# Rows of two token blocks turned by VectorE and a DRAM scratch, and five unused products in the first quad

## The chip, the cores and the metric

The kernel runs on one core of one Trainium2 chip. Its engines are TensorE (PE; the loading of its weights is shown apart as PEld), VectorE (DVE), ScalarE (ACT), GpSimd (POOL) and SyncE (SP), which only issues DMAs here. Each engine works through its own queue in the order in which the program was written for it. The metric is device time in microseconds (us) of one execution, and the median of several runs.

## The reference

One transformer block on 2048 tokens of width 576, in float32: adaptive LayerNorm, grouped attention with 32 query heads of 18 and one shared key and value head, then a channel MLP of 4608.

```python
mod = (_silu(c) @ w_mod).reshape(c.shape[0], 6, 1, -1)
sa, ca, ga, sb, cb, gb = (mod[:, 0], mod[:, 1], mod[:, 2], mod[:, 3], mod[:, 4], mod[:, 5])
h = _layernorm(x, axis=-1) * (1 + ca) + sa
x = x + ga * _A_ref(h, A_wq, A_wk, A_wv, A_wo)
h = _layernorm(x, axis=-1) * (1 + cb) + sb
x = x + gb * _B_ref(h, B_w1, B_b1, B_w2, B_b2)
```

`_A_ref` projects h to 32 query heads, one key head and one value head, takes softmax of the scores times 18 ** -0.5, and projects the result; `_B_ref` is LayerNorm, a dense layer, GELU and a second dense layer.

## The kernel before

The order of the instructions is written out by hand (`manual_schedule`): what stands in the program for an engine is run in that order, and waits on other engines are put in by semaphores. There are three parts: projections of q, k and v (up to about 128 us), attention (to about 1370 us) and the MLP. The change is in the first part and at the head of the second.

**First part.** The 2048 tokens are four blocks `tb` of 512, each of four tiles `t` of 128 tokens. LayerNorm of a tile is done by `ln1_stats` (DVE statistics, three small POOL rows) and `ln1_apply` (ACT or DVE writes the normalised tile to Z, 128 tokens x 576). The projection needs h with the 576 channels on the partitions: five groups `k` of 128 channels (the last one has 64, held twice). `h_chunk(tb, zt, k)` turns four 128x128 pieces of Z with four PE transposes into a psB buffer, and `h_evac` scales them: ACT writes `hf`, ACT writes the rounded high part (`big<-hf`), and POOL or DVE the low part. A product is taken in three terms (high x high, low x high, high x low), so a `q_chunk` of 126 or 128 output columns is 14 products of 512 columns (`proj`).

A block has five such chunks, in the order m = 4, 0, 1, 2, 3 (`i` = 0 to 4). Behind each chunk ACT copies psB to `qf` and `qs`, POOL makes the low part of `qs`, and SP stores it to DRAM (`qscr`). m = 4 holds v and k; behind m = 0 the block's keys and values are finished (`k_block`, `v_block`). The block loop places other work at each `i`:

- h of the next block: `h_chunk` of k = 0, 1, 2 behind `i` = 1 and of k = 3, 4 behind `i` = 2 (in block 0 behind 3 and 4);
- normalising ahead (`NAPPLY`): block 2's tiles 0 and 1 at the end of block 0 and 2 and 3 behind block 1's `i` = 0; block 3's tiles 0 and 1 behind block 1's `i` = 3, and 2 and 3 behind `i` = 4;
- score products of quad 0 for its row maxima (`smax_part`), which are called in the middle of a chunk (`mid`): two psA buffers get two products each, and DVE takes their maxima (L346).

psB has three buffers in this part and psA two; Z has one.

**Second part.** It goes over 32 quads (4 heads x 512 tokens). In each quad scores are taken (`S0`, `S1`, L962), ACT takes their exponential (L964), the value products are summed (`V`, L952, into psC), and for the next quad row maxima are taken (`M0`, `M1`, L321 into three psM buffers, then DVE L984). The strings QUAD, QUADW and LAST fix the order of these tokens. In the first quad the first `LAG` = 8 quarter steps of V have no value products to do, since these follow the exponentials by two steps; so nothing but S and M stands there. Groups 0 and 1 use rows 0 to 63 and 64 to 127 of the array.

Of the kernel before, what the change touches and what calls it, by code (L numbers as in the profile page):

```python
# [8 lines left out]
F32 = mybir.dt.float32  # L9
# [5 lines left out]
S, D, H, DH, F = 2048, 576, 32, 18, 4608  # L15
NB = 4
TB = S // NB
NT = TB // 128
KD = 5
# [13 lines left out]
def block_kernel(ctx: ExitStack, tc, x, wqkv, wo, w1, b1, w2, b2, c, wmod, ident_in, out):  # L33
    nc = tc.nc
    ve, ac, po, pe, sy = nc.vector, nc.scalar, nc.gpsimd, nc.tensor, nc.sync

    per = ctx.enter_context(tc.tile_pool(name="per", bufs=1))
    dr = ctx.enter_context(tc.tile_pool(name="dr", bufs=1, space=bass.MemoryType.DRAM))
# [14 lines left out]
    def psB(): return PS["t"].tile([128, 512], F32, name="psB", bufs=PS["b"])  # L53
    def psC(): return PS["t"].tile([128, 512], F32, name="psC", bufs=1)

    open_ps("1", 3)
    def big(): return per.tile([128, 10, 512], F32R, name="big", bufs=3)
# [10 lines left out]
    w2sum = dr.tile([NG, 128, 4, 2, 288], F32, name="w2sum")  # L68
    turned = [dr.tile([D, 128], F32, name="turned%d" % n) for n in range(2)]
    turned0 = dr.tile([D, 128], F32, name="turnedA")  # L70
    qscr = dr.tile([NB, 2, H * DH, TB], F32, name="qscr")


# [11 lines left out]
    KS = pa.tile([128, S], F32R, name="KS")  # L85
# [3 lines left out]
    p1 = ph1.__enter__()  # L89
# [66 lines left out]
    def tr(o, Z, k):  # L156
        pe.transpose(o, Z[:, 128 * k:128 * (k + 1)], ident)
# [14 lines left out]
    Zs = {}  # L172
# [10 lines left out]

    def ln1_apply(tb, t, e):
        if t == 0:
            Zs[tb] = p1.tile([128, NT, 640], F32, name="Z1")
        Z = Zs[tb]
        X = XT[:, NT * tb + t, :]
        rs, nb = RN.pop((tb, t))
        for o, i in ((Z[:, t, :D], X), (Z[:, t, D:], X[:, 512:])):  # L190
            if e is ac:
                ac.activation(o, i, AF.Identity, scale=rs, bias=nb)
            else:
                ve.tensor_scalar(o, i, rs, nb, op0=ALU.mult, op1=ALU.add)

    mcol = p1.tile([128, 2, KD], F32, name="mcol")

# [29 lines left out]
    def h_evac(p, zt, k, e, first=False):  # L227

        hf = p1.tile([128, TB], F32, name="hf", bufs=3)
        ac.activation(hf, p, AF.Identity, scale=mcol[:, 1, k:k + 1], bias=mcol[:, 0, k:k + 1])  # L230
        if first:
            ve.tensor_copy(zt[:, k, :], hf)
        else:
            ac.activation(zt[:, k, :], hf, AF.Copy)
        e.tensor_tensor(zt[:, KD + k, :], hf, zt[:, k, :].bitcast(F32), op=ALU.subtract)

    def h_chunk(tb, zt, k):
        p = psB()
        for t in range(NT):
            tr(p[:, 128 * t:128 * (t + 1)], Zs[tb][:, t, :], k)  # L240
        h_evac(p, zt, k, ve if tb == 1 and k in (1, 3, 4) else po, tb == 1 and k < 3)

    def proj(o, wh, wl, c0, c1, zt, mid=None, n=0):
# [28 lines left out]
    def q_chunk(tb, m, zt, mid, n):  # L272

        w = 126 if m < KD - 1 else 128
        wd = 126 if m < KD - 1 else 72
        pq = psB()
        proj(pq[:w], wqh, wql, 126 * m, 126 * m + w, zt, mid, n)
        qs = p1.tile([128, 2, TB], F32R, name="qs", bufs=2)
        qf = p1.tile([128, TB], F32, name="qf", bufs=2)
        ac.activation(qf[:w], pq[:w], AF.Copy)  # L280
        ac.activation(qs[:w, 0], pq[:w], AF.Copy)
        po.tensor_tensor(qs[:w, 1], qf[:w], qs[:w, 0].bitcast(F32), op=ALU.subtract)
        if m == KD - 1:
            if tb >= 2:
                key_diff(tb, qf)
        sy.dma_start(qscr[tb, :, 126 * m:126 * m + wd, :].rearrange("s p t -> p s t"), qs[:wd].bitcast(F32))
        return qf, qs

    def k_block(tb, qs):

        pk = psB()
        for i in range(2):
            pe.matmul(pk, pick[:, i, :], qs[:, i, :], start=(i == 0), stop=(i == 1))
        ac.activation(KS[:, TB * tb:TB * (tb + 1)], pk, AF.Identity, bias=ones)

    def v_block(tb, qf):
        pk = psB()
        for i in range(NT):
            pe.transpose(pk[:, 128 * i:128 * (i + 1)], qf[:, 128 * i:128 * (i + 1)], ident)
        ve.tensor_copy(V[:, NT * tb:NT * (tb + 1), :DH],  # L300
                       pk.rearrange("p (i c) -> p i c", i=NT)[:, :, 72:72 + DH])
# [68 lines left out]
    for t in range(NT):  # L370
        ln1_stats(0, t)
        if t:
            ln1_apply(0, t - 1, ve if t % 2 else ac)
# [31 lines left out]
    def dense(n, w, x):  # L405

        p = psB()
        for _ in range(n):
            pe.matmul(p, w, x, start=True, stop=True)
# [35 lines left out]
    def unit():  # L445
        nonlocal u1
        smax_half(1, u1 % 2, u1 // 2)
        u1 += 1
# [5 lines left out]
    for tb in range(NB):  # L454
        nz = big() if tb + 1 < NB else None
        for i, m in enumerate((4, 0, 1, 2, 3)):
            np_ = NPART[tb][i]
            if i == 2:
                parts.extend((u, tb) for u in range(8))
            mid = {(NB - 1, 1): unit, (NB - 1, 4): lambda: last.popleft()()}.get((tb, i), part)  # L460
            qf, qs = q_chunk(tb, m, zt, mid, np_ + 1 if np_ else 0)
            if i == 0:
                qv = qf, qs
            if i == 1:
                k_block(tb, qv[1])
                v_block(tb, qv[0])
                if tb == 0:
                    load_q(0)
            if i == 2:
                if tb == 0:  # L470
                    load_q(1)
            if tb == NB - 1:
                if i == 0:
                    unit()
                elif i == 3:
                    smax_fin1(0)
                if i == 4:
                    dense(5, wqh[:, 0, :128], KS[:, :512])
                    unit()
                    dense(4, wqh[:, 0, :128], KS[:, :512])  # L480
            if nz is not None:
                for k in {1: (0, 1, 2), 2: (3, 4)}.get(i, ()) if tb else {3: (0, 1, 2), 4: (3, 4)}.get(i, ()):
                    h_chunk(tb + 1, nz, k)
            if tb < 2:
                for _ in range(NAPPLY[tb][i]):
                    b, t = applies.popleft()
                    ln1_apply(b, t, ve if b == 1 and t % 2 else ac)
                for _ in range(NSTAT[tb][i]):
                    ln1_stats(*stats.popleft())
        zt = nz  # L490
# [422 lines left out]
    LAG = 8  # L913
# [95 lines left out]

    part = deque((0, 1))  # L1010
    pq = 0
    for n in range(NQT):
        ns = [0, 0]
        if n < NQT - 1:
            order = QUADW if n > NQ else QUAD
        else:
            order = LAST
        if n < NQT - 1:
            kf, kr = (sum(int(tok[1]) for tok in order[:order.index(a)] if tok[0] == "V") // 4 for a in ("F2", "RC"))
            quiet = kf - 2, kf - 1, kr - 1  # L1020
        for tok in order:
            if tok[0] == "V":
                g = int(tok[1:])
                while g:
                    i = min(g, 4 - pq % 4)
                    if pq >= LAG:
                        pv_mm(*divmod((pq - LAG) // 4, 16), pq % 4, pq % 4 + i)
                    pq, g = pq + i, g - i
                    if pq % 4 == 0:
                        between(*divmod(pq // 4 - 1, 16))  # L1030
            elif tok[0] == "S":
                g = int(tok[1])
                two = sum(ns) % 7 % 2 if n == NQT - 1 else ns[g] % 2 and n == NQT - 2 and ns[g] > 24
                st_mm(n, ns[g] // 2, g, ns[g] % 2, psM if two else psB)
                ns[g] += 1
            elif tok in maxima:
                unit = next(maxima[tok], None)
                if unit:
                    mx_mm(*unit, tok[0], int(tok[1]))
            elif tok == "WO":  # L1040
                wo_next(psB)
            elif tok == "WP":
                h2 = part.popleft()
                p = psB()
                wo_mm(NB - 1, 2, h2, p, 0, KD - 1, KD - 1)
                wo_add(NB - 1, 2, h2, p)
            elif tok == "RW":
                for i, w in enumerate("hl"):
                    sy.dma_start(WO[w][:, KD - 1, :].bitcast(F32), woscr[i])
            elif tok[0] == "F":  # L1050
                (smax_fin1 if tok == "F1" else smax_fin2)(n + 1)
            elif n:
                if next(posts[0], 0) == 0:
                    posts.pop()
        if n == NQT - 1:
            W1["r"] = per.tile([128, 40, 128], F32R, name="w1a", tag="big", bufs=3)
            load_w1(0, " ".join(OPS) + " tails")
# [482 lines left out]
```

## Time and profile before

| | |
|---|---|
| runs | 2213.18, 2213.26, 2213.31 us; median 2213.26 |
| the profiled execution | 2214.96 us, with a span of 2212.9 us from its first to its last instruction |
| granted TensorE clock, mean | 0.998 |
| DMA packets | 233528, 317.67 MB |

The profile names a group of instructions by line, engine, operation and tiles (out<-in). In a timeline a row is start, duration, line, what is done and how often, and in brackets the idle time ahead of it and what ended it. In a table of stretches a row gives the stretch, its length, and for each engine the busy time (instructions), then the granted TensorE clock, the mean busy share of the 16 DMA engines, and GB/s.

### The profile page before, as it was taken

The page shows a single profiled execution, that of the slowest core. Times are in us where ns is not written, and L with a number is a line of the kernel's source. Part 1 is how long each engine was busy: PE and PEld are TensorE (multiplying, and loading weights), DVE is VectorE, ACT ScalarE, POOL GpSimd, SP SyncE. Part 2 cuts the span into 40 slices and gives each one's busy share as a digit, 9 for nine tenths or more (in the row PEclk, how much of TensorE's full clock was granted, in tenths as well). Part 3 has the DMA queues.
Part 4 walks back from the last instruction along what each step waited for, and adds up shares of the span by engine and source line. Part 5 has one row for each costly group of instructions (what it writes and reads, how often), then busy time and mean ns, then how long its engine had stood idle before and what let it go on. Part 6 is the DMA issues. An engine that isn't in the chain of part 4 may idle for free.

```text
span 2212.9 us, 46091 instructions
## 1 busy us (share of the span) xinstructions
PE 2193.5 (99%) x16559; PEld 1441.7 (65%) x16559; DVE 1935.3 (87%) x3421; ACT 1626.0 (73%) x3114; POOL 1520.2 (69%) x1760
## 2 busy tenths in 40 slices
PE   8999999999999999999999999999999999999999
PEld 6654445454544445444454445898988899889898
DVE  7589999999999999999999992888888878787887
ACT  5569999999999999999999998544445444343443
POOL 7654356667777677678675640888899767877776
PEclk9999999999999999999999999999999999999999
DMA  6232143333433443443343321666767746676664
GB/s 228 88 134 93 34 132 119 132 128 114 138 124 128 127 138 103 126 141 117 122 128 124 125 71 59 200 195 190 201 186 202 208 131 179 184 217 189 178 183 124
DMA packets 233528, 317.67 MB, mean 144 GB/s; under 512 B 58351, under 2 KB 124287, under 8 KB 233301
## 3 DMA queue, kind: packets, MB, share of 16 engines
q1 hardware_dynamic: 233157, 314.59, 46.4%
q8 instruction: 131, 2.15, 0.4%
q14 instruction: 96, 0.79, 0.1%
q10 hardware_dynamic: 144, 0.15, 0.0%
HBM read 205.92 MB, written 98.51 MB: 138 GB/s over the span
## 4 chain that ended last, share of the span: by engine, by line
PE 93%; DVE 1%; ACT 1%; issue 0%; ACTq 0%; DVEq 0%
PE psC L952 24%; PE psB L1176 18%; PE psA L1279 16%; PE psB L962 14%; PE psM L321 13%; PE psB L751 2%; PE psB L972 2%; PE psA L1313 1%; PE psA L751 1%; PE psB L250 0%; PE psB L359 0%; PE psM L962 0%; ACT P L964 0%; DVE mx L346 0%; DVE gs L1188 0%; ACT h L1185 0%
## 5 line engine op out<-in xcount | busy, mean ns | idle before, releaser
L964 ACT ACTIVATE P<-psB 128x512 f32<-128x512 f32 x2013 | 1055.6, 621 | 49.0 <-PE psM L321 24.4
L984 DVE TENSOR_REDUCE mx<-psM 128x1 f32<-128x512 f32 x1476 | 930.5, 681 | 27.6 <-PE psM L321 12.9
L962 PE MATMUL psB<-qst,KS 64*128 64x512 f32 x2013 | 604.8, 434 | 0.1
L321 PE MATMUL psM<-KS,qst 64*128 64x512 f32 x1722 | 594.0, 435 | 0.7 <-DVE mx L339 0.3
L952 PE MATMUL psC<-P,V 128*32 128x256 f32 (+3 forms) x6608 | 569.0, 440 | 0.0
L962 PEld LDWEIGHTS psB<-qst,KS 64*128 64x128 f32 x2013 | 302.1, 184 | 215.7 <-ACT P L964 184.6
L321 PEld LDWEIGHTS psM<-KS,qst 64*128 64x128 f32 x1722 | 285.4, 184 | 190.1 <-DVE mx L984 140.9
L1176 PE MATMUL psB<-ops,w1a 128*128 128x512 f32 x1512 | 393.9, 396 | 0.2 <-DVE h L1191 0.2
L1176 PEld LDWEIGHTS psB<-ops,w1a 128*128 128x128 f32 x1512 | 270.1, 188 | 46.8 <-DVE h L1191 0.6
L952 PEld LDWEIGHTS psC<-P,V 128*32 128x32 f32 x6608 | 147.1, 108 | 188.5 <-issue 160.9
L1285 DVE TENSOR_TENSOR XT<-psA,XT 128x576 f32<-128x576 f32 x330 | 241.2, 751 | 16.4 <-PE psA L1279 11.0
L1279 PEld LDWEIGHTS psA<-w2s,big 128*128 128x128 f32 x1584 | 223.6, 188 | 12.1 <-DVE XT L1285 0.2
L1279 PE MATMUL psA<-w2s,big 128*128 128x288 f32 x1584 | 230.1, 294 | 0.0
L1253 POOL TENSOR_TENSOR big<-s,big 128x512 fp32r<-128x512 f32 x132 | 170.9, 1295 | 10.6
L982 DVE CUSTOM_DVE_ANT_0 xc<-psM,xc 128x512 f32<-128x512 f32 x246 | 165.6, 680 | 11.8 <-PE psM L321 4.5
L1185 ACT ACTIVATE h<-psB,b1t 128x512 f32<-128x512 f32 x144 | 97.9, 680 | 105.7 <-PE psB L1176 99.3
L1189 ACT ACTIVATE psB<-gs 128x512 f32<-128x512 f32 x144 | 86.7, 602 | 119.9 <-DVE gs L1188 119.9
L975 ACT ACTIVATE xc<-psB 128x512 f32<-128x512 f32 x246 | 154.3, 627 | 5.5 <-PE psM L321 1.9
L788 POOL TENSOR_TENSOR os<-O,os 128x512 fp32r<-128x512 f32 x31 | 39.8, 1285 | 169.6 <-ACT os L787 169.5
L1188 DVE SCALAR_TENSOR_TENSOR gs<-psB,h 128x512 f32<-128x512 f32 x144 | 98.7, 686 | 38.7 <-ACT psB L1186 38.6
L822 POOL TENSOR_TENSOR r<-r,r 128x256 fp32r<-128x256 f32 (+1 forms) x162 | 121.8, 752 | 13.0
L1194 ACT ACTIVATE big<-h 128x512 fp32r<-128x512 f32 x39 | 24.7, 634 | 139.5 <-DVE h L1191 139.5
(215 smaller groups left out, 3289.2 us busy)
## 6 DMA issues: line engine op xcount, KB each, us to landing
w1a<-w1scr SPq DMA_DIRECT2D x252, 256.0 KB
w2s<-w2sum SPq DMA_DIRECT2D x132, 288.0 KB
w1scr<-r SPq DMA_DIRECT2D x126, 256.0 KB
w2s<-w2scr SPq DMA_DIRECT2D x76, 288.0 KB
w2scr<-r SPq DMA_DIRECT2D x72, 288.0 KB
w2sum<-r SPq DMA_DIRECT2D x72, 288.0 KB
qst<-qscr SPq DMA_DIRECT2D x192, 72.0 KB
w1a<-w2scr SPq DMA_DIRECT2D x33, 288.0 KB
```

Source lines behind the costliest of these rows:

```text
L321: pe.matmul(o, QST[n][64 * g:64 * g + 64, p, 128 * qt:128 * (qt + 1)], KS[64 * g:64 * g + 64, 512 * kb:512 * (kb + 1)], start=True, stop=True)
L822: po.tensor_tensor(o[:, n:2 * n], src, o[:, :n].bitcast(F32), op=ALU.subtract)
L952: pe.matmul(PVt[n][32 * j:32 * (j + 1), cs], V[:, kc, :], t[:, j, cs], start=(kc == 0 and h0 == 0), stop=(kc == 15), skip_group_check=True)
L962: pe.matmul(t, KS[64 * g:64 * g + 64, 128 * kc:128 * (kc + 1)], QST[n][64 * g:64 * g + 64, i, :], start=True, stop=True)
L964: ac.activation(P[n, kc][:, 2 * i + g, :], t, AF.Exp, scale=SCALE)
L975: ac.activation(XC[-1], t, AF.Relu)
L982: ve.tensor_tensor_reduce(c, t, c, 1.0, -3.0e38, ALU.add, ALU.max, o)
L984: ve.tensor_reduce(o, t, axis=AX.X, op=ALU.max)
L1176: pe.matmul(o, x, y, start=(first and i == 0), stop=(i == len(terms) - 1), skip_group_check=True)
L1253: po.tensor_tensor(unit(u, 1), x, unit(u, 0).bitcast(F32), op=ALU.subtract)
L1279: pe.matmul(p[:, i, :288], x[:, ts_], W2S[k][:, y], start=(bool(first) and q == 0), stop=(q == 2), skip_group_check=True)
L1285: ve.tensor_tensor(o, p[:, :, :288], o, op=ALU.add)
```

## The change

For blocks 2 and 3 the rows are no longer turned by PE. `ln1_apply` writes Z without its second 64 columns; DVE turns each tile in place, 32x32 squares at a time (`ve.transpose`); behind every second tile SP stores the squares to a scratch in DRAM (`hscr`), eight DMAs with lines of 128 bytes; and `h_load` brings the turned rows back over Z in three DMAs, behind `i` = 1. `h_chunk` then reads them from there instead of from psB, and stands one chunk later (behind `i` = 2 and 3). Z gets two buffers. In the first quad, five products that nobody reads stand ahead of the maxima's products.

```diff
+    hscr = [dr.tile([D, TB], F32, name="hscr%d" % n) for n in range(2)]
...
-            Zs[tb] = p1.tile([128, NT, 640], F32, name="Z1")
+            Zs[tb] = p1.tile([128, NT, 640], F32, name="Z1", bufs=2)
...
-        for o, i in ((Z[:, t, :D], X), (Z[:, t, D:], X[:, 512:])):
+        for o, i in ((Z[:, t, :D], X), (Z[:, t, D:], X[:, 512:]))[:1 if tb > 1 else 2]:
...
+        if tb > 1:
+            ve.transpose(Z[:, t, :D], Z[:, t, :D])
+            if t % 2:
+                for p in range(0, 128, 32):
+                    for i in (t - 1, t):
+                        sy.dma_start(hscr[tb % 2][:, 128 * i + p:128 * i + p + 32].rearrange("(c f) n -> f c n", f=32),
+                                     Z[p:p + 32, i, :D].rearrange("f (c n) -> f c n", n=32))
+
+    def h_rows(tb):
+
+        return Zs[tb].rearrange("p t c -> p (t c)").rearrange("p (k n) -> p k n", n=TB)
+
+    def h_load(tb):
+
+        H, scr = h_rows(tb), hscr[tb % 2]
+        sy.dma_start(H[:, :KD - 1], scr[:512].rearrange("(k p) n -> p k n", p=128))
+        for q in range(2):
+            sy.dma_start(H[64 * q:64 * q + 64, KD - 1], scr[512:])
...
     def h_chunk(tb, zt, k):
-        p = psB()
-        for t in range(NT):
-            tr(p[:, 128 * t:128 * (t + 1)], Zs[tb][:, t, :], k)
+        if tb > 1:
+            p = h_rows(tb)[:, k]
+        else:
+            p = psB()
+            for t in range(NT):
+                tr(p[:, 128 * t:128 * (t + 1)], Zs[tb][:, t, :], k)
...
-                for k in {1: (0, 1, 2), 2: (3, 4)}.get(i, ()) if tb else {3: (0, 1, 2), 4: (3, 4)}.get(i, ()):
+                if tb and i == 1:
+                    h_load(tb + 1)
+                for k in {2: (0, 1, 2), 3: (3, 4)}.get(i, ()) if tb else {3: (0, 1, 2), 4: (3, 4)}.get(i, ()):
...
+    idle = psC()
...
             elif tok in maxima:
+                if n == 0 and 3 <= pq < LAG and tok[0] == "M":
+                    pe.matmul(idle, KS[:64, :128], KS[:64, :512], start=True, stop=True)
```

The first place is DVE in block 1, from the maxima of the chunk m = 2 to the first of block 2. Before, with L346 the maxima of psA and L145 to L150 the statistics of a tile of block 3:

```order
L346 TENSOR_REDUCE mx_600<-psA 128x2 x2
L145 BN_STATS bst<-XT 128x6
L149 BN_STATS bst<-XT 128x6
L150 BN_AGGR mv_800<-bst 128x2
L346 TENSOR_REDUCE mx_600<-psA 128x2 x6
```

Now, with L368 for the maxima, L146 to L151 for the statistics and Z_791 for block 3's Z:

```order
L368 TENSOR_REDUCE mx_610<-psA 128x2 x2
L197 STREAM_TRANSPOSE Z_791<-Z_791 128x576 x2
L146 BN_STATS bst<-XT 128x6
L150 BN_STATS bst<-XT 128x6
L151 BN_AGGR mv_804<-bst 128x2
L368 TENSOR_REDUCE mx_610<-psA 128x2 x2
L197 STREAM_TRANSPOSE Z_791<-Z_791 128x576 x2
L368 TENSOR_REDUCE mx_610<-psA 128x2 x4
```

Two turns of block 3 stand between the maxima of pair 4 and those of pair 5 (one pair of psA buffers to each chunk, counted from block 1's first), and two more behind pair 5. The first two turns of block 2 stand in the same way ahead of pair 1's maxima, the other two behind them.

The second place is ACT in block 1, ahead of block 3's first normalisations. Before (L230 and L234 are an h chunk, L280 and L281 qf and qs, Z_795 is block 3's Z):

```order
L230 ACTIVATE hf<-psB,mcol 128x512
L234 ACTIVATE big<-hf 128x512
L280 ACTIVATE qf<-psB 126x512
L281 ACTIVATE qs<-psB 126x512
L192 ACTIVATE Z_795<-XT,nb_625,rs_624 128x576
L192 ACTIVATE Z_795<-XT,nb_625,rs_624 128x64
L192 ACTIVATE Z_795<-XT,nb_701,rs_700 128x576
```

Now (L249 and L253 are an h chunk, L302 and L303 qf and qs; Z_585 is block 2's Z, which holds the rows brought back, and Z_791 block 3's):

```order
L302 ACTIVATE qf<-psB 126x512
L303 ACTIVATE qs<-psB 126x512
L249 ACTIVATE hf<-Z_585,mcol 128x512
L253 ACTIVATE big<-hf 128x512
L249 ACTIVATE hf<-Z_585,mcol 128x512
L253 ACTIVATE big<-hf 128x512
L193 ACTIVATE Z_791<-XT,nb_643,rs_642 128x576
L193 ACTIVATE Z_791<-XT,nb_695,rs_694 128x576
```

The last two h chunks of block 2 now stand behind the qf and qs of the chunk m = 2, between these and block 3's first normalisations; the first three moved in the same way behind the qf and qs of m = 1.

The third place is SP, from the q store of block 0's m = 1 to block 1's last. Before:

```order
L286 DMA qscr<-qs 126x2x512
L317 DMA qst<-qscr 18x2x512 x6
L286 DMA qscr<-qs 126x2x512 x2
L286 DMA qscr<-qs 72x2x512
L286 DMA qscr<-qs 126x2x512 x4
```

Now (hscr_71 is block 2's scratch):

```order
L308 DMA qscr<-qs 126x2x512 x2
L201 DMA hscr_71<-Z_585 32x18x32 x8
L308 DMA qscr<-qs 72x2x512
L201 DMA hscr_71<-Z_585 32x18x32 x8
L308 DMA qscr<-qs 126x2x512
L211 DMA Z_585<-hscr_71 128x4x512
L213 DMA Z_585<-hscr_71 64x512 x2
L308 DMA qscr<-qs 126x2x512 x2
```

Sixteen stores stand among the q stores of block 0's last chunk and of block 1's m = 4 and m = 0, and three loads behind them. On PE the two runs of transposes (12 and 8) are gone from blocks 1 and 2, and a product into psC stands ahead of each of five L321 rows of the first quad.

## The prediction

> **What bounds the kernel now.** I read the page first, for the engine that carries the span:
>
> ```profile
> PE 2193.5 (99%) x16559; PEld 1441.7 (65%) x16559; DVE 1935.3 (87%) x3421; ACT 1626.0 (73%) x3114; POOL 1520.2 (69%) x1760
> ...
> PE 93%; DVE 1%; ACT 1%; issue 0%; ACTq 0%; DVEq 0%
> ```
>
> TensorE (PE) is busy 99% of the span and 93% of the chain that ended last. Whatever PE is spared in the first part is therefore gained, and whatever it is made to wait is lost, unless PE waits at that place already. So I read PE's timeline in the first part (start, duration, line, count). Tiles are named as in the code; blocks are numbered 0 to 3 and "pair n" is the nth group of four score products into the two psA buffers since block 1 began, one to a chunk, so that pair 6 lies in block 2's first chunk.
>
> ```profile
> 52.77 0.73 PE L321 MATMUL psA<-KS,qst 64*128 64x512 f32 x4
> 56.57 1.53 PE L157 MATMUL psB<-ident,Z 128*128 128x128 f32 x12 [0.33 <-DVE V L300]
> 62.30 1.03 PE L157 MATMUL psB<-ident,Z 128*128 128x128 f32 x8
> 63.70 1.90 PE L250 MATMUL psB<-big,wA 128*126 128x512 f32 x7 [0.36 <-ACT qs L281]
> 66.19 3.50 PE L250 MATMUL psB<-big,wA 128*126 128x512 f32 x14
> 73.72 0.73 PE L321 MATMUL psA<-KS,qst 64*128 64x512 f32 x4
> 74.38 3.51 PE L250 MATMUL psB<-big,wA 128*128 128x512 f32 x14
> 81.59 1.53 PE L157 MATMUL psB<-ident,Z 128*128 128x128 f32 x12 [0.34 <-ACT qs L281]
> 87.33 1.04 PE L157 MATMUL psB<-ident,Z 128*128 128x128 f32 x8
> 88.73 1.89 PE L250 MATMUL psB<-big,wA 128*126 128x512 f32 x7 [0.36 <-ACT qs L281]
> ```
>
> PE runs through here with waits of 0.3 to 0.4 us. A chunk of projection is 14 products of 0.245 us (3.43 us from 66.19 to 69.62) and one pair of 0.66: 4.1 us. Blocks 1 and 2 have five chunks each (m = 4, 0, 1, 2, 3).
>
> **What is removed.** Twice 12 transposes (1.53 us) and 8 transposes with the wait behind them (62.30 to 63.70 and 87.33 to 88.73: 1.40): 2 x 2.93 = 5.86 us of PE, all on the path. The 0.33 us before the 12 stays, since the next chunk needs the same psB buffer. ACT loses eight 64-column rows, which are off the path.
>
> **What is put in their place, on DVE.** Each tile gets a turn of 128x576, and pair 1's maxima now stand behind two of them.
>
> ```profile
> 49.74 2.28 ACT L192 ACTIVATE Z<-XT,nb,rs 128x576 f32<-128x576 f32 x4
> ...
> 50.49 2.34 DVE L346 TENSOR_REDUCE mx<-psA 128x2 f32<-128x1024 f32 x2
> ...
> 52.76 0.44 DVE L145 BATCH_NORM_STATS2 bst<-XT 128x6 f32<-128x288 f32 x1
> ...
> 53.79 2.30 DVE L346 TENSOR_REDUCE mx<-psA 128x2 f32<-128x1024 f32 x2
> ...
> L615 DVE STREAM_TRANSPOSE Z<-Z x8: 767/768/769, 577.6 to 1126.1; 128x576 f32<-128x576 f32 x8
> ```
>
> The four normalisations of 49.74 become two (0.86 us each, next one 0.75 later), so the first is ready at 50.6 and the second at 51.35; the turns end at 52.15, the two maxima at 53.35 and 54.5. PE's pair 2 stands at 52.77 and needs both buffers: it ends its last product at 54.87 instead of 53.44. This 1.43 us and block 1's first 1.53 cancel: chunk m=1 starts at 58.0 (before: 58.09), m=2 at 62.1, m=3 at 66.2, and block 2's first chunk at 70.3 (before: 72.0).
>
> **The way through DRAM.** SP now has 16 stores of 72 KB and 3 loads (1.31 MB) per block, in one queue with the q stores. A store of the same shape (lines of 128 bytes) is in the second stage; the rows show four of them with nothing else behind, a q store of 504 KB whose landing released the load at 37.21, the q store that stands ahead of the new ones, and what big transfers reach:
>
> ```profile
> 1126.88 2.00 SPq L618 DMA_DIRECT2D turnedA<-Z  x4
> ...
> 1128.90:1129.90 1.00, 1.00 (x10) 0.16 (x6) 0.96 (x3) 1.00 (x4) 0.92 (x2) 1.00 0.83 143
> 1129.90:1130.90 1.00, 1.00 (x11) 0.47 (x14) 0.86 (x4) 1.00 (x4) 0.86 (x3) 1.00 0.01 1
> ...
> 34.02 0.31 SPq L286 DMA_DIRECT2D qscr<-qs  x1
> 37.21 2.09 SPq L317 DMA_DIRECT2D qst<-qscr  x6
> ...
> 52.95 0.31 SPq L286 DMA_DIRECT2D qscr<-qs  x1
> ...
> 140.00:145.00 5.00, 5.00 (x59) 3.01 (x59) 4.96 (x11) 5.00 (x11) 5.00 (x4) 1.00 1.05 388
> ```
>
> Four stores took 2.00 us to issue and their packets ended 1.0 us after the last issue (DMA share 0.83, then 0.01). So 16 take some 8.2 us: eight from 53.3 to 57.4, a q store, eight to 61.9, a q store to 62.2. The load waits until the last of the 16 has landed: its packets end at 62.9. The q store of 34.02 took 3.2 us until it released the load, 1.3 of them data at 388 GB/s, so 1.9 lie ahead of the packets and behind them; with a third of that behind them (a choice, no row parts them) the load goes at 63.5. Its main part (1.05 MB at 388 GB/s: 2.7 us, and 1.9) lands at about **68.0**. Bounds: stores that issue in 0.31 us like the q stores give 65.2; the q store's data ahead of the load (1.3) and the last store landing 3.2 us after its issue (1.1 later) give 70.4. I take 68.0, since the row of the same shape gives the issue. Behind the new stores on SP stand only the q stores of the next chunks: that of m=0 goes at 62.2 instead of 58.2, and its buffer is written again by ACT's m=2, later still.
>
> **What waits for it.** ACT's queue has the five h chunks of block 2, then the normalisations of block 3, in order.
>
> ```profile
> 57.26 0.78 ACT L230 ACTIVATE hf<-psB,mcol 128x512 f32<-128x512 f32 x1
> ...
> 58.61 0.76 ACT L230 ACTIVATE hf<-psB,mcol 128x512 f32<-128x512 f32 x1
> ...
> 62.56 0.60 ACT L280 ACTIVATE qf<-psB 126x512 f32<-126x512 f32 x1 [1.19 <-PE psB L250]
> ...
> 69.09 2.28 ACT L192 ACTIVATE Z<-XT,nb,rs 128x576 f32<-128x576 f32 x4
> ...
> 70.17 2.36 DVE L346 TENSOR_REDUCE mx<-psA 128x2 f32<-128x1024 f32 x2 [0.70 <-PE psA L321]
> ```
>
> A chunk is 1.34 us there (57.26 to 58.61), qf and qs 0.97. ACT is through with m=1 at 63.4 and then idles for the load. From 68.0: three chunks 4.02, qf and qs 0.97, two chunks 2.68, end 75.7; block 3's first two normalisations, which ran at 69.09 before, are ready at 76.5 and 77.3. DVE's queue has their turns ahead of pair 5's maxima (70.17 before): turns to 78.1, statistics 1.03 (52.76 to 53.79), maxima at 80.3 and 81.45. PE stands at pair 6, in the middle of block 2's first chunk (73.72 before), from about 72.5 on: its two halves go at 80.4 and 81.55, and the chunk ends at 83.6 instead of 76.1 (74.38 + 7 x 0.245). That is 7.5 us late. POOL's low parts of h, 1.32 us each, end by 78.7 and are hidden in this wait; so is the late q store. From there PE saves 2.93 us with block 2's transposes: **4.6 us late** at block 3. Block 3's own load comes about 1 us after ACT asks for it (stores end at 87.3, the q store of m=0 is ready about 91, landing 95.5), but its first chunk begins only at 103, so nothing is added.
>
> ```profile
> 58.78 3.96 POOL L235 TENSOR_TENSOR big<-hf,big 128x512 fp32r<-128x512 f32 x3 [0.64 <-ACT big L234]
> ```
>
> **The clock, and the five products.** What PE's idling costs beside the time shows at the first quad:
>
> ```profile
> 131.93 0.49 PE L321 MATMUL psM<-KS,qst 64*128 64x512 f32 x1
> 131.93 0.50 PE L962 MATMUL psB<-qst,KS 64*128 64x512 f32 x1
> ...
> 134.66 1.93 PE L952 MATMUL psC<-P,V 128*32 128x512 f32 x8
> ...
> 137.81 1.07 PE L952 MATMUL psC<-P,V 128*32 128x512 f32 x8
> ...
> 131.30:133.70 2.40, 2.08 (x9) 0.86 (x9) 2.40 (x5) 2.39 (x6) 0.00 (x0) 1.00 0.70 192
> 134.00:137.40 3.40, 3.40 (x15) 0.99 (x15) 1.47 (x4) 1.79 (x5) 0.00 (x0) 0.50 1.02 359
> 137.40:140.80 3.40, 3.40 (x29) 1.16 (x27) 3.31 (x6) 3.10 (x7) 1.69 (x1) 1.00 1.05 390
> ```
>
> From 131.3 to 133.7 DVE and ACT are full and PE starts only two products per 0.6 us, at one time; then the granted clock is 0.50 for 3.4 us, and eight products take 1.93 us instead of 1.07. That is at most 3.4 / 2 = 1.7 us lost. The five unused products, 0.25 us each, stand where PE waits for DVE's maxima, so they cost nothing while that wait covers them (without it, 1.25). If they hold the clock the loss goes: **-1.5**, between +1.25 and -1.7. The new stall of block 2 leaves PE without work from 72.5 to 80.4, longer than the thin stretch that brought the clock down; I take the same price, **+1.7** (0 to 3.4).
>
> The Trainium skill, "TensorE: Matmul & The Clock Gate", section "Part 1: The HAM clock gate", says that activity is judged in free-running windows of about 3.4 us, that an idle window halves the clock and only a busy one restores it. The 3.4 us at 0.50 agree. By the rule, the window in which PE resumes would not count as busy, so that the price of the stall would be an estimated 2.2 us instead of 1.7 (the fourth rival's working), and the sum below 5.3 instead of 4.8.
>
> **The sum.** +4.6 + 1.7 - 1.5 = +4.8 us on the profiled execution's 2214.96 us: 2219.8. The median of the runs shown is 2213.26, 1.7 lower; the same sum on it gives **2218.1 us** (+0.22%). The second Z buffer and POOL's later rows cost nothing: POOL is idle behind them. A difference of 0.2% (4.4 us) is what a measurement can tell from none.
>
> **Rivals.** First, *the load is early enough and it comes out even*: every microsecond of landing is a microsecond of the end, until 63.4, where ACT no longer waits. Then ACT's own chain sets pair 6 (block 3's turns end at 73.5, maxima at 75.7 and 76.9): block 2's first chunk ends at 79.0, 2.9 us late, which its transposes pay back, PE's gap is under 4 us, and without a clock drop 2213.26 - 1.5 = 2211.8 remain. With a landing at 66.5 and the drop it is 3.1 + 1.7 - 1.5 = +3.3: 2216.6. For it speaks that the q stores issue in 0.31 us; against it, that four stores of this shape took 2.00. The landing from which it decides against 4.4 us is 67.6. Chance 0.40.
>
> Second, *PE is simply spared*: nothing waits, -5.86 - 1.5 = -7.4, 2205.9. Against it stands the order alone: block 3's turns are ahead of pair 5's maxima on DVE and behind all five chunks of block 2 on ACT, whenever the load lands. Chance 0.08, with all else that is faster by over 0.2%.
>
> Third, *the five products don't hold the clock*: 4.6 + 1.7 = +6.3, 2219.6. The stretch is thin since DVE and ACT are full in it (2.40 and 2.39 of 2.40), and five products of 0.25 add 1.2 us to PE's work in it; no row shows how much is enough. Chance 0.10.
>
> Fourth, *the clock comes back later after the stall*. The 3.4 us at 0.50 were busy throughout (3.40 of 3.40); where PE resumes it has four products with a wait between them, and if only a full stretch brings the clock back, those four take 0.5 us longer (half of the 1.0 is hidden in the wait) and 1.7 follow: 4.6 + 2.2 - 1.5 = +5.3, 2218.6. Chance 0.12. The section of the skill named above states this rule.
>
> **How the numbers follow.** The forecast itself has 0.30, and with the third and fourth rival slower by over 0.2% has 0.52; within 0.2%: 0.40; faster: 0.08. The range goes from the first rival's best (2211.8, set to 2211.5) to a landing at 70.4 with a clock that comes back late and products that hold it (4.6 + 2.4 + 2.2 - 1.5 = +7.7, 2221.0) and half of the products' failing beside it (2221.7), set to 2222.5 for waits too small to list; some 0.15 is left outside. The forecast's own range is 2216.5 to 2222.
>
> **What would show it.** Right: no transposes of Z for blocks 2 and 3; a PE gap of 7 to 9 us ahead of pair 6, ended by the maxima of psA, and behind it a granted clock of 0.5; ACT idle from about 63 until the DMA of Z at about 68; DVE idle ahead of the turns of block 3, ended by ACT; no 0.50 after 134 plus the shift. Wrong: ACT's hf of block 2 running by 64, or pair 6 within 4 us of chunk m=3's end; or a clock drop in the first quad beside the five products.

## The result and the profile after

| | before | after |
|---|---|---|
| median of five runs | 2213.31 us (2213.18 to 2214.33) | 2226.14 us (2225.16 to 2226.67) |
| ratio | | 1.0056, 95% interval 1.0042 to 1.0071 |
| the profiled execution, and its span | 2214.96, 2212.9 us | 2225.59, 2223.6 us |
| granted clock, mean | 0.998 | 0.995 |

The change costs 12.8 us, where 4.8 were predicted; 2226.14 lies outside the range (2211.5 to 2222.5). The page of after has the same bound, with a little less on PE and a new name in the chain:

```profile
PE 2191.3 (99%) x16524; PEld 1439.1 (65%) x16524; DVE 1940.4 (87%) x3429; ACT 1623.4 (73%) x3106; POOL 1521.2 (68%) x1760
...
PE 93%; DVE 2%; ACT 2%; DMA 2%; issue 1%; POOL 0%; SPq 0%; ACTq 0%; DVEq 0%; POOLq 0%
```

DMA has 2% of the chain now. The chain in order of time (start, duration, what) says where; these are its pieces of DMA and DVE of over 1.8 us from 60 to 110 us:

```profile
63.13 1.99 DMA hscr<-Z
65.39 6.73 DMA Z<-hscr
...
83.46 2.23 DVE mx L368 x2
...
97.80 7.74 DMA Z<-hscr
```

The last store of block 2 lands 1.99 us after its issue begins, the load takes 6.73 us behind it, and block 3's load stands in the chain as well, with 7.74 us. The timeline of after between them (L201 stores, L211 the load, L249 ACT's first h row, L197 a turn, L272 projections, L343 pairs, L368 maxima):

```profile
53.17 4.91 SPq L201 DMA_DIRECT2D hscr<-Z  x8
58.72 4.94 SPq L201 DMA_DIRECT2D hscr<-Z  x8
65.39 0.39 SPq L211 DMA_DIRECT2D Z<-hscr  x1
...
72.20 0.81 ACT L249 ACTIVATE hf<-Z,mcol 128x512 f32<-128x512 f32 x1 [8.82 <-DMA Z<-hscr]
...
80.91 1.54 DVE L197 STREAM_TRANSPOSE Z<-Z 128x576 f32<-128x576 f32 x2 [14.24 <-ACT Z L193]
...
57.83 1.89 PE L272 MATMUL psB<-big,wA 128*126 128x512 f32 x7 [0.33 <-ACT qs L303]
...
73.73 0.49 PE L272 MATMUL psB<-big,wA 128*128 128x512 f32 x1 [3.32 <-ACT big L253]
84.60 0.79 PE L343 MATMUL psA<-KS,qst 64*128 64x512 f32 x2 [6.50 <-DVE mx L368]
86.46 5.68 PE L272 MATMUL psB<-big,wA 128*128 128x512 f32 x14
111.53 0.73 PE L343 MATMUL psA<-KS,qst 64*128 64x512 f32 x4
113.77 0.96 PE L272 MATMUL psB<-big,wA 128*128 128x512 f32 x3 [0.61 <-POOL big L254]
115.44 0.73 PE L343 MATMUL psA<-KS,qst 64*128 64x512 f32 x4
146.82 1.06 PE L976 MATMUL psC<-P,V 128*32 128x512 f32 x8
148.71 1.06 PE L976 MATMUL psC<-P,V 128*32 128x512 f32 x8
```

The waits are the predicted ones, in the predicted order: ACT waits for the DMA of Z, DVE for ACT's normalisation, PE for DVE's maxima. The gap ahead of pair 6 is 6.50 us, not 7 to 9, since PE already stands for 3.32 us ahead of the chunk's first product, which needs the late h. Pair 6 starts at 84.60 instead of 73.72 (+10.9), the 14 products behind it at 86.46 instead of 74.38 (+12.1). The two pairs around block 3's first seven products stood here before:

```profile
100.30 0.74 PE L321 MATMUL psA<-KS,qst 64*128 64x512 f32 x4
...
102.79 1.20 PE L321 MATMUL psA<-KS,qst 64*128 64x512 f32 x4
```

The first is 11.2 us late (111.53) and the second 12.6 (115.44), since PE waits for POOL's low parts between them. The first value products of attention are 12.2 late (146.82 against 134.66), the second ones 10.9 (148.71 against 137.81). After that the difference stays within 0.2 us up to the end.

The granted clock (seventh figure, behind the five busy times and the length) in stretches of after:

```profile
74.20:84.50 10.30, 3.05 (x7) 1.66 (x6) 3.49 (x7) 9.03 (x15) 8.91 (x11) 0.50 0.28 72
84.40:87.80 3.40, 2.86 (x7) 1.72 (x8) 3.40 (x5) 0.87 (x1) 1.52 (x3) 0.50 0.74 145
87.80:91.20 3.40, 3.40 (x9) 2.62 (x9) 1.46 (x2) 1.09 (x2) 0.19 (x1) 0.50 1.05 223
```

It is 0.50 through the stall and up to 91.2, 6.6 us behind its end, though PE works again there (2.86 and 3.40 of 3.40 us). In the first quad it is 1.00 throughout.

### The profile page after: what moved, and what is told of

Its sections match the earlier page's. It is cut to its first block, busy times and chain, and to the rows that moved or that the text cites. A ratio compares the mean times of both kernels' runs of the same rounds, so it can differ in the third digit from the quotient of the medians.

```text
span 2223.6 us, 46063 instructions
## 1 busy us (share of the span) xinstructions
PE 2191.3 (99%) x16524; PEld 1439.1 (65%) x16524; DVE 1940.4 (87%) x3429; ACT 1623.4 (73%) x3106; POOL 1521.2 (68%) x1760
## 4 chain that ended last, share of the span: by engine, by line
PE 93%; DVE 2%; ACT 2%; DMA 2%; issue 1%; POOL 0%; SPq 0%; ACTq 0%; DVEq 0%; POOLq 0%
PE psC L976 24%; PE psB L1203 18%; PE psA L1306 16%; PE psB L986 14%; PE psM L343 13%; PE psB L775 2%; PE psB L996 2%; PE psA L1340 1%; PE psB L272 1%; DMA Z<-hscr 1%; PE psA L775 1%; DVE mx L368 1%; DMA bigw<-in_wmod 0%; ACT hf L249 0%; PE psB L381 0%
## 5 line engine op out<-in xcount | busy, mean ns | idle before, releaser
L343 PE MATMUL psM<-KS,qst 64*128 64x512 f32 x1722 | 593.2, 434 | 0.4 <-DVE mx L361 0.3
L343 PEld LDWEIGHTS psM<-KS,qst 64*128 64x128 f32 x1722 | 285.1, 184 | 188.9 <-DVE mx L1008 139.7
L1306 PEld LDWEIGHTS psA<-w2s,big 128*128 128x128 f32 x1584 | 223.6, 188 | 12.2 <-DVE XT L1312 0.2
```

The lines of the kernel that those rows point to most:

```text
L343: pe.matmul(o, QST[n][64 * g:64 * g + 64, p, 128 * qt:128 * (qt + 1)], KS[64 * g:64 * g + 64, 512 * kb:512 * (kb + 1)], start=True, stop=True)
L1306: pe.matmul(p[:, i, :288], x[:, ts_], W2S[k][:, y], start=(bool(first) and q == 0), stop=(q == 2), skip_group_check=True)
```

## The experiments

Times are medians of five to eleven runs, and each ratio is to runs of the kernel before on the same chip. The medians of the kernel before differ by up to 1 us between chips, so where a time is set against after's, about 1 us is open. "Ahead" and "late" of a first part compare the same instruction with the first profile of the kernel before.

### What the half clock in the first quad is worth

Three runs: after without the five products, before with them alone, and the kernel before once more.

```diff
-                if n == 0 and 3 <= pq < LAG and tok[0] == "M":
-                    pe.matmul(idle, KS[:64, :128], KS[:64, :512], start=True, stop=True)
```

> The changed kernel without the five unused products. Theory (they hold the clock where DVE and ACT leave PE thin): the 12.2 us by which the first value products were late (134.66 to 146.82) and the 10.9 us by which the fourth group was late (141.88 to 152.78) differ by 1.3, so without them about 1.5 us is lost again: 2227.7 us, with a granted clock of 0.5 for 3.4 us between 143 and 152. Rival (the drop is a matter of where the stretch falls in time, and the products did nothing): 2226.1, with or without a drop.

Measured 2225.87 us (2224.75 to 2227.50), ratio 1.0058 (1.0045 to 1.0070). The same as after, as the rival has it. Its profile has no half clock where the products are missing:

```profile
146.00:149.40 3.40, 3.40 (x27) 1.20 (x27) 2.91 (x5) 3.05 (x7) 0.00 (x0) 1.00 1.04 349
```

> The kernel before with the five unused products alone. Theory: the 3.4 us at half clock from 134 go, -1.5 us: 2211.8. Rival 1 (the products have no cover and hold nothing): +1.2, 2214.5. Rival 2 (they only move the drop to a later stretch): 2213.3.

Measured 2213.32 us (2213.07 to 2213.86, 11 runs), ratio 0.9999 (0.9990 to 1.0007): no gain. The granted clock is 1.00 there:

```profile
134.00:137.40 3.40, 3.40 (x26) 1.06 (x25) 2.93 (x6) 3.25 (x7) 0.00 (x0) 1.00 1.04 325
```

> The kernel before, unchanged, profiled a second time. Theory (the half clock at 134 in the first profile comes in some executions only, by where a 3.4 us window falls): the profiled execution takes about 2213.3 us instead of 2214.96 if the granted clock stays at 1.0 there, and again about 2215 if it doesn't. Rival (the drop is in every execution, and the first profile was 1.7 us long for another reason): 0.5 at 134 and 2213.3 together.

The kernel before, unchanged, in the same stretch of its second profile, an execution of 2213.46 us:

```profile
134.00:137.40 3.40, 3.40 (x27) 1.01 (x26) 2.91 (x6) 3.25 (x7) 0.00 (x0) 1.00 1.03 371
```

1.00, where the first profile (2214.96 us) has 0.50. From there on the second profile is 1.5 us ahead of the first. So the drop comes in some executions only, and PE's busy time ahead of it doesn't tell them apart: from 130.6 to 134.0 PE was busy for 2.93 of 3.40 us in the first profile and for 2.92 in the second. The ten runs of this kernel fall into two groups, 2213.19 to 2213.46 (four) and 2214.55 to 2215.14 (six), their means 1.6 apart. That the upper group is the one with the drop is read from two profiles alone.

That the five products hold the clock is not shown by a profile, since the two without them here have no drop either. For it speaks that no time of eleven with them was over 2213.86, while six of 21 of the kernel before on that chip were over 2214; against it, that two of the versions below with block 3 alone, which have them too, show times in two groups as well, whatever the reason. From a median that lies in the lower group they can take nothing.

### Block 3 alone, block 2 alone

`tb > 1` becomes `tb > 2`, or `tb == 2`; the other block is turned by PE at its old place.

> The changed kernel with block 2 turned by PE again, at its old place; block 3 keeps DVE's turns, the stores and the load; the five products stay. Theory (block 2's late load starts the loss, through ACT's order, and the clock follows it): no stall ahead of pair 6 beyond 1 us, no 0.5 near 74 us; block 3's transposes are saved (-2.9), the products give -1.5, block 3's load costs up to 0.9: 2209 to 2211, say 2210. Rival (any block that goes through DRAM costs a stall of its own size, by the turns on DVE and the stores on SP): half of the loss, about 2219.

Measured 2212.94 us (2211.91 to 2214.47), ratio 0.9998 (0.9989 to 1.0007). There is no stall at block 2 and no half clock near 74, as the theory has it, but the gain is missing. Its timeline:

```profile
74.78 0.50 PE L343 MATMUL psA<-KS,qst 64*128 64x512 f32 x2 [0.59 <-DVE mx L368]
101.32 0.97 PE L272 MATMUL psB<-big,wA 128*128 128x512 f32 x3 [0.99 <-POOL big L254]
...
93.20 0.82 ACT L249 ACTIVATE hf<-Z,mcol 128x512 f32<-128x512 f32 x1 [5.21 <-DMA Z<-hscr]
...
82.85 1.30 SPq L308 DMA_DIRECT2D qscr<-qs  x2
84.97 0.39 SPq L211 DMA_DIRECT2D Z<-hscr  x1
```

Of the 2.93 us, 0.8 go at pair 6, whose second half waits for maxima behind the turns (the 14 products behind it start at 75.22 instead of 74.38). The load goes at 84.97 behind two q stores and is used at 93.20, 8.2 us later. Block 3's first chunk begins 1.9 us ahead, then PE waits for POOL (0.99, and 0.27 a little later) and is on a par behind it. So a load that is late by 5 us for ACT eats the rest.

> The changed kernel with block 3 turned by PE again, at its old place; block 2 keeps DVE's turns, the stores and the load; the five products stay. Theory (block 2's load reaches PE through the low parts of h, whatever stands on DVE): the chunk m=4 of block 2 ends near 84 instead of 89.9, the clock is at half for part of the time to 91, chunk m=1 starts 9 us later than in the kernel before, and nothing is added: 2222.3 (2221 to 2223.5). Rival 1 (block 2's stall comes from block 3's turns, which are gone here): block 2 comes out even, 2213 to 2215. Rival 2 (the whole loss is block 2's): 2226.

Measured 2220.74 us (2220.47 to 2221.53), ratio 1.0030 (1.0019 to 1.0042): between the rivals, and just below the theory's range. Pair 6 no longer waits (no turns stand ahead of its maxima), and PE waits for POOL's low parts instead; the first of the eight products at 82.54 ends the chunk m=4:

```profile
77.71 1.22 PE L343 MATMUL psA<-KS,qst 64*128 64x512 f32 x4
81.29 0.96 PE L272 MATMUL psB<-big,wA 128*128 128x512 f32 x3 [0.79 <-POOL big L254]
82.54 2.12 PE L272 MATMUL psB<-big,wA 128*128 128x512 f32 x8 [0.28 <-POOL big L254]
```

From m=1 on the first part is 7.4 us late, up to its end. So of the 12.4 in after, 7.4 are block 2's load by itself, with its own stretch of half clock, and 5 come with block 3, net of the 2.93 that block 3 saves.

### Block 3's turns later

```diff
-    NAPPLY = ((0, 2, 2, 0, 2), (2, 0, 0, 2, 2))
+    NAPPLY = ((0, 2, 2, 0, 2), (2, 0, 0, 0, 4))
```

> The changed kernel with all four normalisations and turns of block 3 behind the last chunk of block 1, so that pair 5's maxima don't stand behind two of them on DVE. Block 2's load stays where it is. Theory (the late load reaches PE through ACT's order and the turns ahead of the maxima): pair 6 waits no longer for DVE; PE then waits only for the low parts of block 2's h, whose last ends near 82, so the chunk m=4 of block 2 ends near 83 instead of 89.9; block 3's load lands only some 4.6 us earlier and gives part of that back: 2221 (2219 to 2222.5). Rival (the load alone holds PE, through the low parts of h, and the order on DVE hides behind that): 2226, no change.

Measured 2226.05 us (2224.97 to 2226.94), ratio 1.0056 (1.0042 to 1.0069): no change, as the rival has it, but not for the rival's reason.

```profile
77.56 0.86 PE L343 MATMUL psA<-KS,qst 64*128 64x512 f32 x4
92.66 1.90 PE L272 MATMUL psB<-big,wA 128*126 128x512 f32 x7 [0.24 <-ACT qs L303]
...
106.47 0.81 ACT L249 ACTIVATE hf<-Z,mcol 128x512 f32<-128x512 f32 x1 [6.01 <-DMA Z<-hscr]
```

Pair 6 goes at 77.56 without a wait (84.60 in after), and the chunk m=4 ends near 85.5 instead of 92.1, so that it was not the load alone that held it. But the four turns now stand ahead of pair 6's maxima, so that pair 7 waits for these (0.98 and 0.62 us at 86.5), and the half clock falls on the chunk m=0 (0.52 from 88 to 91); m=1 of block 2 is only 3.2 us earlier (92.66 against 95.84). All of that is given back at block 3, whose 16 stores now go in one piece and whose load is used at 106.47, 0.8 later than in after. Two loads stand one behind the other here, and with the first wait shortened the second one sets nearly the same end.

### The clock of the stall alone

46 unused products fill PE's gaps at block 2's first chunk; every wait for data stays.

```diff
+            if (tb, i) == (2, 0):
+                rest(12)
...
+            if n < 0 and i in (0, 3):
+                rest(4)
...
+    def part_rest():
+        rest(26)
+        part()
```

> The changed kernel with 46 more unused products of 0.25 us where PE stands still at block 2's first chunk: 12 ahead of it (the 3.3 us gap), 4 and 4 between its first seven products, 26 ahead of pair 6 (the 6.5 us gap). All data waits stay. Theory: the granted clock stays at 1.0 from 74 to 91 us, and pair 6's second half and the 14 products behind it are no longer at half speed: -2.7 us, and block 3's load, which goes behind the q store of m=0, moves with them: 2223.4 (2222.5 to 2224.5). Rival 1 (the end is set by block 3's load whatever the clock does): 2226. Rival 2 (the products have too little cover and push pair 6): 2227.

Measured 2223.25 us (2222.99 to 2225.03), ratio 1.0043 (1.0030 to 1.0056): 2.9 below after, as expected. This run's clock in the stall and behind it, and the 14 products:

```profile
74.20:84.10 9.90, 9.90 (x40) 6.73 (x39) 3.52 (x7) 8.63 (x14) 8.55 (x12) 1.00 0.30 77
84.20:91.20 7.00, 6.36 (x28) 4.32 (x29) 6.11 (x7) 1.95 (x3) 3.28 (x4) 1.00 0.93 189
...
85.73 3.52 PE L284 MATMUL psB<-big,wA 128*128 128x512 f32 x14
```

The 14 products behind pair 6 take 3.52 us instead of 5.68, and from pair 6's start (84.17) to the next pair it is 5.0 us instead of 7.5. So the half clock behind the stall is worth 2.5 us there, not 1.7. The other 0.4 is pair 6's own start, which follows a load that was used 0.45 us earlier. In the profile block 3's load gives 0.9 back (PE waits 0.99 and 0.27 us for POOL), and the first part ends 2.0 earlier than after's. How long the half clock lasts behind such a stall differs: in four other runs with the stall (after without the five products, the load ahead of the q stores, and the two with half of the stores) the 14 products take 4.79, 6.06, 6.13 and 4.78 us.

### The load ahead of the q stores

`h_load` stands behind `i` = 0 instead of 1.

> The changed kernel with each load of turned rows placed behind the first chunk of a block (i = 0) instead of the second: on SP's queue it then stands ahead of the q store of m=0, not behind it. It still waits for the last of the 16 stores. Theory (the load took 6.8 us to land since 504 KB of q rows went just ahead of it and as many behind it): block 2's load goes at the same 65.4 and lands about 1.4 us earlier, near 70.8; block 3's goes at 93.5 instead of 97.8, lands near 100, and the 0.9 us that PE waits for POOL there goes: 2223.8. Rival (1.31 MB take 6.8 us by themselves): only the 0.9 goes, 2225.2.

Measured 2224.10 us (2222.78 to 2224.38), ratio 1.0043 (1.0030 to 1.0057). The number is the theory's, half of its mechanism is not:

```profile
65.34 0.38 SPq L211 DMA_DIRECT2D Z<-hscr  x1
92.98 0.38 SPq L211 DMA_DIRECT2D Z<-hscr  x1
...
71.70 0.81 ACT L249 ACTIVATE hf<-Z,mcol 128x512 f32<-128x512 f32 x1 [8.33 <-DMA Z<-hscr]
101.18 0.82 ACT L249 ACTIVATE hf<-Z,mcol 128x512 f32<-128x512 f32 x1
```

Block 2's load still takes 6.4 us (65.34 to 71.70) with no q store just ahead of it. With that store in its place, 1.6 us ahead, it takes 6.8 in after, but 6.2, 6.3, 6.5 and 6.6 in four other runs (the 46 products, block 3's turns later, after without the five products, block 2 alone), so that no cost of the store can be told, let alone 1.4. Block 3's load goes 4.8 us earlier than in after, ACT doesn't wait for it (101.18, straight behind its own work), PE's waits for POOL are gone, and the first part is 11.1 us late instead of 12.4, with 0.1 of the 1.3 there ahead of block 3. So block 3's load costs 1.2 us in after.

### Block 2's load earlier: two misses

Half of block 2's stores are left out (every second group of 32 tokens by the edit, not of channels); rows of x are copied into the scratch ahead of it, so that block 2's h is not the true one.

```diff
-                for p in range(0, 128, 32):
+                for p in range(0, 128, 64 if tb == 2 else 32):
...
+                    sy.dma_start(hscr[0], x[:D, :TB])
```

> The changed kernel with half of block 2's 16 stores left out (every second group of 32 channels; those rows of the scratch hold rows of x, copied there at about 46 us, so block 2's h is not the true one). Theory (each microsecond by which block 2's load lands later is a microsecond of the end): the last store is issued 2.5 us earlier, the load goes near 63 instead of 65.4 and lands near 69.7 instead of 72.2; pair 6 and all behind it move by 2.5: 2223.6 (2222.5 to 2224). Rival (the end is set by block 3's load, whose stores and wait are unchanged): 2226.

Measured 2225.62 us (2224.38 to 2226.93), ratio 1.0051 (1.0038 to 1.0064). The copy took the queue from the q stores, and ACT stood for one of them. The load went at 63.53, as meant, but 0.6 us behind the next q store, and took 8.3 us; used at 71.81, it was hardly earlier:

```profile
56.46 0.60 ACT L303 ACTIVATE qs<-psB 128x512 fp32r<-128x512 f32 x1 [4.06 <-DMA qscr<-qs]
71.81 0.82 ACT L249 ACTIVATE hf<-Z,mcol 128x512 f32<-128x512 f32 x1 [5.63 <-DMA Z<-hscr]
...
84.22 0.79 PE L343 MATMUL psA<-KS,qst 64*128 64x512 f32 x2 [7.20 <-DVE mx L368]
```

> As the run with half of block 2's stores, with the copy of x into the scratch at about 39 us instead of 46, where in that run it held up a q store, ACT by 4.1 us, and so the load, which landed at 71.8. Theory (pair 6 follows the landing one for one: 84.60 after 72.2, 84.22 after 71.8, 84.09 after 71.7, always 12.4 later): the load goes near 63 and lands near 69.7, pair 6 starts near 82.1, and block 3, whose q store and load come 2.5 us earlier too, keeps that: 2223.6 (2222.8 to 2224.6). Rival (below 71 something else than the landing holds pair 6, and the end doesn't follow): 2225.5 or more.

Measured 2226.35 us (2224.62 to 2227.02), ratio 1.0056 (1.0042 to 1.0070). The copy at 39 us did the same one chunk earlier (ACT waited 3.6 us there, and PE with it, at half clock from 47 to 54). The load went at 63.29, 0.6 us behind a q store that this delay had moved next to it, and took 7.8 us:

```profile
62.73 0.31 SPq L308 DMA_DIRECT2D qscr<-qs  x1
63.29 0.38 SPq L211 DMA_DIRECT2D Z<-hscr  x1
...
71.05 0.81 ACT L249 ACTIVATE hf<-Z,mcol 128x512 f32<-128x512 f32 x1 [4.52 <-DMA Z<-hscr]
...
83.46 0.79 PE L343 MATMUL psA<-KS,qst 64*128 64x512 f32 x2 [7.17 <-DVE mx L368]
```

As tests of a landing at 69.7 both failed, and what a landing below 71 would do is not shown. What they do show, with after and the last two runs above (the 46 products, the load ahead of the q stores): pair 6 starts 12.4 us behind the first use of the load in all five (72.20 and 84.60, 71.75 and 84.17, 71.70 and 84.09, 71.81 and 84.22, 71.05 and 83.46). In that range a microsecond of landing is a microsecond at pair 6. In the last one the first part is 11.2 us late in the profile instead of 12.4, and yet the median is no lower; what its other executions lost isn't known.

### A version that gains: block 3 alone, made early

Normalisations and turns of block 3 one chunk earlier, one statistics step moved, the load behind `i` = 0 of block 2:

```diff
-    NSTAT = ((2, 2, 2, 2, 0), (1, 1, 1, 1, 0))
-    NAPPLY = ((0, 2, 2, 0, 2), (2, 0, 0, 2, 2))
+    NSTAT = ((2, 2, 2, 2, 0), (1, 2, 1, 0, 0))
+    NAPPLY = ((0, 2, 2, 0, 2), (2, 0, 2, 2, 0))
```

> As the run with block 3 alone through DRAM, with block 3's normalisations and turns one chunk earlier (behind i = 2 and 3 of block 1 instead of 3 and 4; one statistics step moved from i = 3 to i = 1) and its load behind i = 0 of block 2. In that run the load went at 85.0, landed at 93.2, and PE waited 1.3 us for POOL's low parts at 101 and lost 0.8 at pair 6. Theory (a load that lands ahead of ACT's need leaves the 2.93 us of transposes as a plain gain): load near 79, landed by 86, no wait of ACT for it: 2210.5 (2209.8 to 2211.5). Rival (the turns on DVE delay the maxima wherever they stand, and PE waits for them): 2212 to 2213.5.

Measured 2212.90 us (2211.26 to 2213.78, 11 runs), ratio 0.9993 (0.9984 to 1.0002) against a kernel before whose median lay in its upper group there (2214.35): not told from no change.

```profile
69.86 0.49 PE L343 MATMUL psA<-KS,qst 64*128 64x512 f32 x2 [1.11 <-DVE mx L368]
70.99 0.50 PE L343 MATMUL psA<-KS,qst 64*128 64x512 f32 x2 [0.64 <-DVE mx L368]
...
88.19 0.81 ACT L249 ACTIVATE hf<-Z,mcol 128x512 f32<-128x512 f32 x1
```

ACT waits for the load no longer, but now PE waits 1.75 us for maxima behind the turns. Both sides were half right: the first part is 1.9 ahead in the profile. But 0.9 of this has nothing to do with the edit: pair 1 is that much ahead already (47.78 against 48.67), behind a start in which the granted clock was 0.99 from 22 to 26 us, against 0.66 in the kernel before. So block 3 gains 1.0 here, and the 1.87 that the next expectation starts from is too much. Then the turns behind the maxima of the next chunk:

```diff
+    def turn_pair(tb, t):
+        part()
+        Z = Zs[tb]
+        for i in (t, t + 1):
+            ve.transpose(Z[:, i, :D], Z[:, i, :D])
...
+                   (1, 3): lambda: turn_pair(3, 0), (1, 4): lambda: turn_pair(3, 2)}.get((tb, i), part)
```

> As the last run with block 3 alone, with each two turns on DVE (and their stores) behind the maxima of the chunk that follows the normalisation, not ahead of them. In that run PE waited 1.1 and 0.6 us for maxima that stood behind the turns, at 69.9 and 71.0, and the rest of the first part was 1.87 us ahead of the kernel before. Theory (the waits at 69.9 and 71.0 are all that the way through DRAM still costs): they go, the first part is 2.9 us ahead, and the time is 1 us below that run: 2210.4 where the first quad of the kernel before loses no clock, against 2213.3 for that kernel. The load goes 2 to 3 us later (near 83) and lands near 89, about 1 us behind ACT's need, which POOL's slack hides. Rival (the later load now costs what the turns cost): no better than that run, 2211.4 or more.

Measured **2209.93 us** (2209.62 to 2210.41, 11 runs), ratio **0.9982 (0.9973 to 0.9990)** to the kernel before (2213.73 beside it), below both kernels.

```profile
68.19 1.43 DVE L201 STREAM_TRANSPOSE Z<-Z 128x576 f32<-128x576 f32 x2
...
69.48 0.74 PE L346 MATMUL psA<-KS,qst 64*128 64x512 f32 x4
97.79 1.89 PE L275 MATMUL psB<-big,wA 128*128 128x512 f32 x7
...
89.73 0.82 ACT L252 ACTIVATE hf<-Z,mcol 128x512 f32<-128x512 f32 x1 [2.72 <-DMA Z<-hscr]
```

The turns fill DVE's idle time, the pair runs with no wait, ACT's wait of 2.72 us reaches no product (seven in 1.89 us, unbroken). The first part is 3.2 us ahead, 0.15 of it ahead of the change (pair 1 at 48.52): the 2.93 of one block's transposes, paid in full. The medians differ by 3.8, with the five products on one side only.

## Why the prediction was wrong

The direction and the chain of waits were right, the size was 8.0 us short. Step by step:

- **Transposes, -5.86.** Right: block 3 alone gives its half (2.93) when nothing waits.
- **First pairs, chunk m=1 at 58.0.** Right to 0.2: 57.83.
- **From the load to pair 6, 12.4 us** (68.0 to 80.4). Right to a tenth, in five runs.
- **The load at 68.0.** This step failed, +4.2. The 16 stores were issued by 63.66 instead of 61.9 (4.91 and 4.94 us for eight, where four of that shape had taken 2.00); the last took 1.99 us to land, and the load went at 65.39 instead of 63.5; it took 6.8 us to its first use instead of 4.5. I had counted its main part alone, 1.05 MB at the full 388 GB/s, with two more loads beside it and q stores on either side; from 65.3 to 72.2 the core's DMA moved 2.0 MB, at 296 GB/s. That the rest of this traffic makes the difference is argued, not shown, since without the q store ahead of it the load still took 6.4. 72.2 lies above even the upper bound (70.4), which had the q store in it but not the rest.
- **Block 3's load adds nothing.** Failed, +1.2 (`h_load` moved), by the same term. The 91 of the prediction for the q store ahead of it, plus the 6.8 us by which chunk m=4 ended later still than forecast (14.3 late, not 7.5), is 97.8, where the load went; but it took 7.8 us instead of 4.5, so that ACT stood for it for 4.21 us instead of about 1. (By the prediction's own 4.6 us the pair of 100.30 would have come at 104.9, and not the chunk at 103; it took too little slack there.)
- **Half clock, +1.7.** Too small: 2.5 in after's profile. Here the fourth rival, with 2.2, was right in kind. The Trainium skill, "TensorE: Matmul & The Clock Gate", section "Part 1: The HAM clock gate", has only a busy window restore the clock; the trace agrees, with 0.50 kept behind 84.4 to 87.8 us, where PE was busy for 2.86 of 3.40, and 1.00 only behind the next 3.40, all of them busy.
- **Five products, -1.5.** This failed on the median. The size of the drop is right (12.2 late ahead of it, 10.9 behind it, against a profile that has it), but the executions at the median have no such drop, with the products or without; that the products hold the clock stays open. The prediction itself noted that the profiled execution was 1.7 us above the median, and half of the 3.4 us at 0.50 is 1.7: it took the gain from a number that already lacked the loss. The same section of the Trainium skill calls the window free-running and its effect different from run to run; the two profiles of the kernel before agree.

On the median then: 4.6 + 4.2 + 2.5 + 1.2 + 0 = 12.5, against 12.8 measured. The clock's 2.5 and block 3's 1.2 come from the profiles of other runs, so that this sum is good to some tenths. The first rival (the load early, even) and the second (PE spared) both needed a load that the runs never had for block 2; with block 3 alone, made early, the second one came true for one block.

## What to carry to other kernels

Before a stretch of half clock in a profile is priced, hold the profiled execution's time against the median: if it is longer by just that price, the execution at the median probably doesn't have the drop. Cost a way through DRAM as a whole chain, from the issue of the last store to the first use of the load, with everything in the same queue around it, and then ask which in-order engine stands at its end and what is queued there behind it. New work on an engine goes behind what others wait for on it: the same turns cost 1.75 us ahead of the maxima and nothing behind them.

## What the runs showed of the hardware

- One program, two profiles, granted clock 0.50 and 1.00 in the same stretch (134.0 to 137.4 us), 1.5 us apart, with PE busy for 2.93 and 2.92 of 3.40 us just ahead of it.
- The same load (1.31 MB, three DMAs) took from issue to first use, by a waiting ACT, 6.2 to 6.8 us with a q store 1.6 us ahead of it (five cases) and 6.4 with none just ahead (one), but 7.7 to 8.7 with one 0.5 to 1.3 us ahead (ten cases).
- Not settled: of block 3 alone, made early, five of eleven times were 2211.26 to 2212.03 and six 2212.90 to 2213.78, and its one profile (2211.26) has the clock at 0.99 from 22 to 26 us, where the first profile of the kernel before has 0.66. Whether the start makes the two groups, no run shows.
